# Output stores of four units with 8 KB rows in a scan and mixture-of-adapters kernel on one core

## The chip, the cores and the metric

The kernel runs on one core of one Trainium2 chip. The metric is the device time in microseconds (us) of one execution; less is better. The profile's span (200.2 us) is a little shorter than the device time, because it begins with the first instruction that the profiler records.

## What is computed

Two stages follow each other. The first is a linear recurrence over 6,400 time steps for 8 sequences of 128 channels; its result, seen as 51,200 rows of 128, goes through a mixture of 8 low-rank adapters of which each row uses its best two.

```python
# a, b: (8, 6400, 128) float32
h = np.zeros((B, D))
for t in range(S):
    h = a[:, t] * h + b[:, t]
    x[:, t] = h                          # x.reshape(51200, 128)
logits = x @ w_gate                      # (51200, 8)
topk = two largest logits of each row
w = softmax(the two logits)
delta = sum over the two e of  w_e * (x @ A[e]) @ B[e]   # A: 128x16, B: 16x128
out = x + delta                          # float32
```

The kernel must read a and b (26.2 MB each) and write out (26.2 MB): 78.6 MB in all, plus 0.14 MB of weights.

## The kernel before

The 51,200 rows are cut into 100 **units** of 512 rows. A unit goes through every engine. A small planner in the file lists all steps of all units as operations with their dependencies, gives each a key (`KEY`, one offset per kind of step), and lays them out as one fixed instruction order for each engine. On the chip each engine then works through its own list and waits on semaphores.

The steps of unit w, with the name that the planner has for each:

```python
load    SyncE    a, b of two units: HBM -> a_in, b_in, 512 KB each, rows of 4 KB
AB      TensorE  16 float32 transposes of a and b into two PSUM banks
aev     ScalarE  a: PSUM -> a_st              (ring of CFG["ast"] = 3)
scan    VectorE  tensor_tensor_scan           -> xT, float16 (ring of XR = 20 units)
ZL      TensorE  xT @ [w_gate | A]            -> PSUM;  zl (ScalarE) moves it to SBUF
gating  VectorE, GpSimd, ScalarE: top two of 8 logits and their weights, for groups of 3 units
mul     GpSimd (a few on VectorE): zw = z * weight
T       TensorE  transposes zw;  tev (VectorE, a few on ScalarE) moves it to SBUF
D       TensorE  x and zwT @ B added up in PSUM
oev     ScalarE  PSUM -> outt                 (ring of NOUT = 24 units)
store   SyncE    outt -> out, HBM
```

Rows go to partitions so that a store's rows are whole runs in HBM: a store of two units takes the 1,024 rows as `(p i) d -> p (i d)` with i = 8, so each of 128 partitions writes 8 rows of 128 floats, 4 KB in a row. For this, the matmul that reads xT picks every eighth row, and D of a unit can only run after the scan of both units of its pair:

```python
def x_block(v, q):
    if v in SOLO:
        x0 = (v % XR) * UT
        return xT[:, x0 : x0 + UT].rearrange("d (p i) -> d i p", i=Q)[:, q, :]
    x0 = (v - v % 2) % XR * UT
    return xT[:, x0 : x0 + 2 * UT].rearrange("d (p i) -> d i p", i=2 * Q)[:, v % 2 * Q + q, :]

def scanned(v):
    return f"scan{v if v in SOLO else v | 1}"

def readers(v):      # who must have read xT before scan(v + XR) writes there again
    both = [v] if v in SOLO else [v - v % 2, v | 1]
    return [f"D{u}" for u in both] + [f"ZL{k}" for u in both for k in fills_of.get(u, [])]
```

The stores. All loads and stores are issued on SyncE, in one order; a store of unit u0 is also held until the scan of unit u0 + HOLD (20), so that the loads go first and some stores are left for the end of the run:

```python
stores = [(u, 2) for u in range(0, NU - 2, 2)] + [(NU - 2, 1), (NU - 1, 1)]

def store(j):
    u0, n = stores[j]
    ...   # cut: source and destination views
    add_dma(f"st{j}", "sp", u0 + HOLD, [(rows, tile)], ("o", s0, n), ns,
            [f"oev{v}" for v in range(u0, u0 + n)] + [f"scan{min(u0 + HOLD, NU - 1)}"])
```

A load of unit w has key w - 16 in the same order and waits for AB of the units that had its place in the ring (8 places of two units, for a and for b). The three weight tensors are loaded on ScalarE's queue.

Of the kernel before, what the change touches and what calls it, by code (L numbers as in the profile page):

```python
# [12 lines left out]
CFG = {  # L13
    "ring": 8,
    "xr": 20,
    "zr": 48,
    "nout": 24,
    "hold": 20,
    "heads": (1, 1, 1, 1),
    "group": 3,  # L20
    "tails": (2, 2, 1, 1),
    "quick": (2, 2),
    "split": (4, 4),
    "solo": (2, 2),
    "mul": (0, 1, 0, 8),
    "tev": (1, 1, 4, 4),
    "tail": 8,
    "heat": 6,
    "filler": (2, 1, 1),
    "caps": {'a': 3, 'b': 4, 'Z': 1, 'O': 3, 'w': 8},  # L30
    "least": {'Z': 1, 'O': 1},
    "pairs": (98, 2),
    "ast": 3,
    "tevns": (264.0, 330.0),
    "key": {
        "AB": 170.4, "aev": 138.5, "scan": 13.3, "ZL": 157.0, "zl": 152.0, "gate": 31.6, "r1": -64.5, "r2": -65.8,
        "sig": 83.8, "mul": 73.7, "T": 119.3, "tev": 143.8, "D": 171.1, "oev": 151.4, "R": 65.1,
    },
}

# [60 lines left out]
class _Plan:  # L101
# [15 lines left out]
    def add(self, name, eng, kind, unit, busy, emit, deps=(), dma=None, mode=None, takes=(), gives=None):  # L117
        self.ops[name] = _Op(name, eng, kind, unit, busy, self.latency, emit, list(deps), dma, mode, takes, gives)
# [161 lines left out]
def bass_associative_scan_2x2__then__mixture_of_adapters_kernel(  # L280
# [8 lines left out]
    NB, S, D = a.shape  # L289
    E = moe_w_gate.shape[1]  # L290
    R = moe_A.shape[2]
# [4 lines left out]
    Q = 4  # L296
    UT = 64 * QI
    assert UT == 128 * Q and N % (2 * UT) == 0 and S >= UT
    NU = N // UT
    RING = CFG["ring"]  # L300
    XR = CFG["xr"]
    NOUT = CFG["nout"]
# [33 lines left out]
    GB = GM * Q  # L336
    SOLO = [v for v in range(NU) if v < CFG["solo"][0] or v >= NU - CFG["solo"][1]]
    assert CFG["solo"][0] % 2 == 0 and CFG["solo"][1] % 2 == 0 and XR % 2 == 0 and NOUT % 2 == 0
    p0, p1 = CFG["pairs"]
    PAIRED = {w: (w - p0) % 2 for w in range(p0, NU - p1)}  # L340
    assert (NU - p0 - p1) % 2 == 0 and p0 >= 2 and p1 >= 1
# [15 lines left out]
    fills_of = {}  # L357
# [11 lines left out]
    with ExitStack() as stack:  # L369
# [4 lines left out]
        cst_f = sb(nc.sbuf_tensor("cst_f", [128, E + 256], F32))  # L374
# [14 lines left out]
        xT = sb(nc.sbuf_tensor("xT", [128, XR * UT], F16))  # L389
        zw = [sb(nc.sbuf_tensor(f"zw{i}", [128, Q, 128], F16)) for i in range(NZW)]  # L390
        zwT = [sb(nc.sbuf_tensor(f"zwT{i}", [128, UT], F16)) for i in range(NZT)]
        zl = sb(nc.sbuf_tensor("zl", [128, ZR, E_A], F32))
        outt = sb(nc.sbuf_tensor("outt", [128, NOUT, UT], F32))
# [26 lines left out]
        def add_dma(name, eng, unit, starts, slot, ns, deps=(), kind="dma", issue=450.0, after=2000.0):  # L420

            if slot not in dma_sem:
                dma_sem[slot] = [sb(nc.semaphore("q_" + "_".join(map(str, slot)))), 0]
            dma_sem[slot][1] += 16 * len(starts)
            sem, value = dma_sem[slot]

            def emit(h):
                for dst, src in starts:
                    last = h.dma_start(dst, src).then_inc(sem, 16)
                return last  # L430

            add(name, eng, kind, unit, issue * len(starts), emit, deps, (sem, value, ns, after))
# [10 lines left out]
                out=ident_f[:, :],  # L443
# [7 lines left out]
            ["id0"],  # L451
        )

        add_dma("wg_in", "act", -110, [(cst_f[:, 0:E], moe_w_gate[:, :])], ("wg",), 80.0, (), "fix", 450.0, 2000.0)
        add_dma(
            "A_in",
            "act",
            -109,
            [(cst_f[:, E : E + 128], moe_A.rearrange("e (h l) r -> (e h) (l r)", l=8))],
            ("A",),  # L460
            220.0,
# [5 lines left out]
        add_dma(  # L467
            "B_in",
            "act",
            -108,  # L470
            [(cst_f[:, E + 128 : E + 256], moe_B.rearrange("e r d -> (e r) d"))],
            ("B",),
            220.0,
# [9 lines left out]
        def heat(h):  # L483
            for _ in range(CFG["heat"]):
# [13 lines left out]
                out=high[:, :], in_=ident_f[:, :].rearrange("p (e h) -> p h e", e=E), axis=AX.X, op=ALU.max  # L498
# [22 lines left out]
                out=mine[:, :], in_=ident_f[:, :].rearrange("p (e h) -> p e h", e=E), axis=AX.X, op=ALU.max  # L521
# [4 lines left out]
        for name, eng, lo, hi, time in (("spr0", "pool", 0, 3, 900.0), ("spr1", "dve", 3, 8, 760.0)):  # L526
# [7 lines left out]
                    out=spread[:, lo:hi, :, :],  # L534
# [61 lines left out]
        def place(t, w):  # L596

            shift = 1 if t == "a" else 0
            half = 64 * ((w + shift) % 2)
            return (w + shift) // 2, slice(half, half + 64)  # L600
# [7 lines left out]
        def column(t, w):  # L608

            return w * UT if t == "b" else 0  # L610

        def load(t, w):

            n = place(t, w)[0]
            many = 1 if (t, w) in alone else 2
            dst, i = rings[t][:, n % RING, :], QI
            if many == 1:
                dst, i = dst[:, column(t, w) : column(t, w) + UT], Q
            src = rows_of[t][w * UT : (w + many) * UT, :].rearrange("(p i) d -> p (i d)", i=i)
            for k in range(many):  # L620
                load_of[t, w + k] = f"ld{t}{w}"
            add_dma(
                f"ld{t}{w}",
                "sp",
                w - 2 * RING + (0 if w > 3 else -200),
                [(dst, src)],
                (t, n % RING, many, w if many == 1 else 0),
                1290.0 if many == 2 else 690.0,
                users.get((t, n - RING), []),
            )  # L630

        def transposes(w):
# [56 lines left out]
            )  # L689

        def readers(v):
            both = [v] if v in SOLO else [v - v % 2, v | 1]
            return [f"D{u}" for u in both] + [f"ZL{k}" for u in both for k in fills_of.get(u, [])]

        def scan(w):
            t0 = w * UT
# [6 lines left out]
            def emit(h):  # L703
# [21 lines left out]
                1187.0 + 130.0 * (len(cuts) - 2),  # L725
                emit,
                [f"AB{w}", f"aev{w}"] + [f"scan{w - 1}"] + readers(w - XR),
                gives=("b", w),
            )


        def x_block(v, q):
            if v in SOLO:
                x0 = (v % XR) * UT
                return xT[:, x0 : x0 + UT].rearrange("d (p i) -> d i p", i=Q)[:, q, :]
            x0 = (v - v % 2) % XR * UT
            return xT[:, x0 : x0 + 2 * UT].rearrange("d (p i) -> d i p", i=2 * Q)[:, v % 2 * Q + q, :]

        def scanned(v):
            return f"scan{v if v in SOLO else v | 1}"  # L740

        def products(k):
            b0, n = fills[k]
# [2 lines left out]
            def emit(h):  # L746
                for j in range(n):
                    dst = bank(("Z", k))[:, j * E_A : (j + 1) * E_A]
                    last = h.matmul(dst, x_block((b0 + j) // Q, (b0 + j) % Q), wA_h)
                return last  # L750
# [206 lines left out]
        def delta(v):  # L957
            def emit(h):
                for part in range(2):
                    for q in range(Q):  # L960
                        cols = slice(q * 128, (q + 1) * 128)
                        last = h.matmul(
                            bank(("O", v))[:, cols],
                            (x_block(v, q), zwT[v % NZT][:, cols])[part],
                            (ident_h[:, :], Bcat_h)[part],
                            start=part == 0 and q == 0,
                            stop=part == 1,
                            skip_group_check=True,
                        )
                return last  # L970

            add(f"D{v}", "pe", "D", v, 485.0, emit, [scanned(v), "idh", f"tev{v}", "cstB"], mode="full")
            plan.ops[f"D{v}"].at = {"cstB": Q}
# [15 lines left out]
                gives=("O", v),  # L989
            )  # L990

        stores = [(u, 2) for u in range(0, NU - 2, 2)] + [(NU - 2, 1), (NU - 1, 1)]
        store_of = {v: j for j, (u0, n) in enumerate(stores) for v in range(u0, u0 + n)}

        def store(j):
            u0, n = stores[j]
            s0 = u0 % NOUT
            rows = out[u0 * UT : (u0 + n) * UT, :]
            tile, ns = outt[:, s0 : s0 + n, :], 680.0 * n
            if u0 in SOLO:  # L1000
                rows = rows.rearrange("(n p i) d -> p n (i d)", p=128, i=Q)
            else:
                rows = rows.rearrange("(p i) d -> p (i d)", p=128)
                tile, ns = tile.rearrange("p n c -> p (n c)"), 1290.0
            add_dma(
                f"st{j}",
                "sp",
                u0 + HOLD,
                [(rows, tile)],
                ("o", s0, n),  # L1010
                ns,
                [f"oev{v}" for v in range(u0, u0 + n)] + [f"scan{min(u0 + HOLD, NU - 1)}"],
            )

        for w in range(NU):
            for t in "ab":
                if (t, w) not in load_of:
                    load(t, w)
# [15 lines left out]
            gating(k)  # L1034
        for j in range(len(stores)):
            store(j)
        ends = [f"st{j}" for j in range(len(stores) - NOUT, len(stores))]
        add("end", "sp", "fix", 1.0e9, 10.0, lambda h: h.nop(), ends)

        plan.schedule()  # L1040
# [49 lines left out]
```

## Time and profile before

| What | Value |
|---|---|
| Time, median of 3 runs | 201.86 us (201.60 to 201.91) |
| Span of the profiled run | 200.2 us |
| TensorE busy | 184.2 us (92%) |
| ScalarE busy | 180.0 us (90%) |
| VectorE busy | 173.8 us (87%) |
| GpSimd busy | 158.5 us (79%) |
| Mean DMA rate over the span | 396 GB/s |

How to read it: four compute engines have a high busy share, and the DMA engines a higher one. Busy time counts an instruction from its start to its end, and instructions of one engine overlap (100 `oev` copies of 625 ns and 100 `aev` copies of 628 ns stand for 61 us each), so a busy share of 90% is not the same as 90% of what the engine can do. The profile also cuts the span into slices and gives for each the share of the time in which the 16 DMA engines were busy and the GB/s that they moved; the share can come out a little over 1, because the packets of one engine overlap slightly.

### The profile page before, as it was taken

The numbers are of one execution on the slowest core, as the hardware profiler recorded it, in microseconds if no ns is written. First come the engines' busy times: TensorE is split into PE (matmuls) and PEld (weight loads), VectorE is DVE, ScalarE is ACT, GpSimd is POOL, SyncE is SP. The second block draws the span as 40 slices with busy tenths as digits, with TensorE's granted clock in tenths as the row PEclk, the third lists the DMA queues.
The fourth block names the chain that finished last, engine by engine and source line by source line (L and its number), as shares of the span: only waits on it lengthen the run. The fifth ranks groups of instructions, "written<-read, shape, count | busy, mean of one in ns | idle before, by whom it ended". The sixth has DMA issues, their size and how long they took to land.

```text
span 200.2 us, 8009 instructions
## 1 busy us (share of the span) xinstructions
PE 184.2 (92%) x3202; PEld 163.2 (82%) x3202; DVE 173.8 (87%) x302; ACT 180.0 (90%) x463; POOL 158.5 (79%) x278
## 2 busy tenths in 40 slices
PE   7599899999999999999989999999999999897760
PEld 3478797899998989999979998898899898796650
DVE  3369999999999999899989889879797999789950
ACT  3159999999999999999999999999999999999770
POOL 2315658889898999988789999999999898887720
PEclk9759999999999999999999999999999999999998
DMA  5999999999999999999999999999999999998994
GB/s 204 352 417 408 410 405 406 408 402 410 403 420 413 414 417 418 413 414 420 410 416 413 414 413 414 421 413 417 418 413 415 413 416 413 412 369 328 407 383 172
DMA packets 22629, 79.30 MB, mean 396 GB/s; under 512 B 2624, under 2 KB 2880, under 8 KB 22592
## 3 DMA queue, kind: packets, MB, share of 16 engines
q1 hardware_dynamic: 22160, 78.65, 97.8%
q8 instruction: 25, 0.41, 0.8%
q10 hardware_dynamic: 432, 0.14, 0.3%
q14 instruction: 12, 0.10, 0.1%
HBM read 52.56 MB, written 26.21 MB: 393 GB/s over the span
## 4 chain that ended last, share of the span: by engine, by line
PE 56%; DVE 22%; ACT 9%; DMA 3%; issue 3%; POOL 3%; POOLq 1%; SPq 0%; DVEq 0%; ACTq 0%
PE ps L94 29%; PE ps L98 28%; DVE xT L710 17%; ACT outt L978 3%; DMA a_in<-in_a_dram 3%; ACT a_st L686 3%; DVE zwT L942 2%; ACT zl L767 2%; POOL zw L926 2%; POOLq L369 1%; POOL d L880 1%; ACT pn L816 1%; DVE zw L926 1%; DVE m L851 1%; DVE m L873 0%
## 5 line engine op out<-in xcount | busy, mean ns | idle before, releaser
L710 DVE TENSOR_TENSOR_SCAN xT<-a_st,xT,ps 128x512 f16<-128x512 f32 x96 | 120.3, 1253 | 12.6 <-PE ps L98 6.2
L926 POOL TENSOR_TENSOR zw<-zl,g 128x512 f16<-128x512 f32 x93 | 99.2, 1072 | 8.5 <-ACT g L905 6.8
L767 ACT COPY zl<-ps 128x408 f32<-128x408 f32 (+1 forms) x139 | 73.0, 532 | 1.6 <-PE ps L94 1.6
L98 PE MATMUL ps<-ident_f,a_in 64*128 64x64 f32 (+1 forms) x792 | 68.7, 232 | 2.2 <-DMA a_in<-in_a_dram 2.2
L98 PE MATMUL ps<-ident_f,b_in 64*128 64x64 f32 (+1 forms) x792 | 67.4, 231 | 0.1
L686 ACT COPY a_st<-ps 128x512 f32<-128x512 f32 x100 | 60.9, 628 | 7.2 <-PE ps L98 6.2
L98 PEld LDWEIGHTS ps<-ident_f,a_in 64*128 64x128 f32 (+1 forms) x792 | 57.5, 141 | 9.5 <-DMA a_in<-in_a_dram 2.7
L978 ACT COPY outt<-ps 128x512 f32<-128x512 f32 x100 | 60.9, 625 | 2.0 <-PE ps L94 1.3
L98 PEld LDWEIGHTS ps<-ident_f,b_in 64*128 64x128 f32 (+1 forms) x792 | 56.5, 141 | 1.2 <-DVE xT L710 0.4
L94 PE MATMUL ps<-cst_h,xT 128*128 128x136 f16 x400 | 51.3, 236 | 1.0 <-DVE xT L710 0.5
L94 PE MATMUL ps<-ident_h,xT 128*128 128x128 f16 x400 | 42.5, 229 | 1.3 <-DVE zwT L942 1.0
L98 PE MATMUL ps<-ident_h,zw 128*128 128x128 f16 x400 | 39.1, 220 | 4.3 <-DVE zw L926 2.0
L94 PEld LDWEIGHTS ps<-cst_h,xT 128*128 128x128 f16 x400 | 36.4, 148 | 6.0 <-DVE xT L710 2.5
L94 PE MATMUL ps<-cst_h,zwT 128*128 128x128 f16 x400 | 38.7, 220 | 0.0
L942 DVE COPY zwT<-ps 128x256 f32<-128x256 f32 x89 | 35.7, 409 | 2.6 <-PE ps L98 2.4
L94 PEld LDWEIGHTS ps<-ident_h,xT 128*128 128x128 f16 x400 | 33.0, 147 | 3.4 <-DVE zwT L942 2.5
L98 PEld LDWEIGHTS ps<-ident_h,zw 128*128 128x128 f16 x400 | 25.0, 98 | 8.4 <-POOL zw L926 3.2
L94 PEld LDWEIGHTS ps<-cst_h,zwT 128*128 128x128 f16 x400 | 27.2, 99 | 0.0
L816 ACT ACTIVATE pn<-d 128x96 f32<-128x96 f32 (+2 forms) x72 | 22.6, 322 | 0.9 <-POOL d L858 0.6
L888 POOL TENSOR_TENSOR d<-d 128x96 f32<-128x96 f32 (+2 forms) x36 | 13.8, 383 | 5.0 <-DVE d L841 4.6
L866 POOL TENSOR_TENSOR L<-zl,pn 128x96 f32<-128x96 f32 (+2 forms) x34 | 12.9, 380 | 5.1 <-ACT pn L816 4.9
L880 POOL TENSOR_TENSOR d<-zl,m 128x96 f32<-128x96 f32 (+2 forms) x34 | 12.2, 359 | 4.7 <-DVE m L873 4.7
(38 smaller groups left out, 90.0 us busy)
## 6 DMA issues: line engine op xcount, KB each, us to landing
a_in<-in_a_dram SPq DMA_DIRECT2D x49, 512.0 KB, 15.3
b_in<-in_b_dram SPq DMA_DIRECT2D x49, 512.0 KB, 15.3
out_dram<-outt SPq DMA_DIRECT2D x49, 512.0 KB, 15.3
a_in<-in_a_dram SPq DMA_DIRECT2D x2, 256.0 KB, 8.9
b_in<-in_b_dram SPq DMA_DIRECT2D x2, 256.0 KB, 4.8
out_dram<-outt SPq DMA_DIRECT2D x2, 256.0 KB, 4.7
cst_f<-in_moe_A_dram ACTq DMA_DIRECT2D x1, 64.0 KB, 3.5
cst_f<-in_moe_B_dram ACTq DMA_DIRECT2D x1, 64.0 KB, 6.2
```

Source lines behind the costliest of these rows:

```text
L94: return self.handle.matmul(*args, **kwargs)
L98: return self.handle.transpose(*args, **kwargs)
L686: lambda h: h.copy(a_st[w % NAS][:, :], bank(("a", w))[:, :]),
L710: last = h.tensor_tensor_scan(out=x_at(lo, hi), data0=a_st[w % NAS][:, lo:hi], data1=bank(("b", w))[:, lo:hi], initial=init, op0=ALU.mult, ...
L767: return h.copy(zl[:, r0 : r0 + n, :], src)
L816: lambda h: h.activation(v(pn[s]), v(src[s]), ACTF.Relu, bias=bias, scale=scale),
L866: lambda h: h.tensor_tensor(out=v(L2[s]), in0=Lg, in1=v(pn[s]), op=ALU.subtract),
L880: lambda h: h.tensor_tensor(out=v(d2[s]), in0=Lg, in1=bc(m2[s]), op=ALU.subtract),
L888: lambda h: h.tensor_tensor(out=v(d1[s]), in0=v(d1[s]), in1=v(d2[s]), op=ALU.add),
L926: lambda h: h.tensor_tensor(out=oview, in0=zview, in1=gview, op=ALU.mult),
L942: return copy(zwT[v % NZT][:, :].bitcast(F32), bank(("O", v))[:, 0 : UT // 2])
L978: return copy(outt[:, v % NOUT, :], bank(("O", v))[:, :])
```

## The change

Stores become blocks of four units for units 4 to 91 (`quads` = (4, 8): not the first four, not the last eight). A block of four takes 2,048 rows with 16 rows to a partition, so each partition writes 8 KB in one run, and one DMA moves 1 MB. The other stores: two pairs at the start, three pairs and two single units at the end. This makes 29 stores in place of 51.

What comes with it:

- D of a unit must wait for the scan of the last unit of its block of four, and a place of xT becomes free only when all four units of its block have been read (`scanned`, `readers`, `x_block` by `block_of`).
- The output ring grows from 24 to 28 units, and `hold` from 20 to 22.
- a_st becomes a ring of 4 in place of 3.
- The weight loads stay on ScalarE's queue, with new keys.
- All keys are set anew, so every engine's list has another order. The split of work is moved a little: one in eight `tev` copies goes to ScalarE in place of all to VectorE; the gating groups at both ends have other sizes; more groups use the short way with `max` (7 in place of 4); the first units have more filler matmuls.

In the instruction lists: VectorE has 79 `tev` copies in place of 89 and 52 `max` in place of 16, ScalarE 21 `tev` copies in place of 11, SyncE 22 stores of 128 x 2048 floats and 5 of 128 x 1024 in place of 48 of 128 x 1024 and one with two 2 KB rows to a partition (units 0 and 1, which `solo` kept apart); the last two units have 128 x 512 in both. The matmuls of the computation are the same in number and shape.

```diff
-    "nout": 24,
-    "hold": 20,
-    "heads": (1, 1, 1, 1),
+    "nout": 28,
+    "hold": 22,
+    "quads": (4, 8),
+    "heads": (1, 2, 1),
     "group": 3,
-    "tails": (2, 2, 1, 1),
-    "quick": (2, 2),
-    "split": (4, 4),
-    "solo": (2, 2),
-    "mul": (0, 1, 0, 8),
-    "tev": (1, 1, 4, 4),
-    "tail": 8,
+    "tails": (2, 1),
+    "quick": (4, 3),
+    "split": (4, 8),
+    "solo": (0, 2),
+    "mul": (0, 1, 0, 10),
+    "tev": (7, 8, 4, 4),
+    "tail": 6,
     "heat": 6,
-    "filler": (2, 1, 1),
+    "filler": (2, 2, 2),
-    "ast": 3,
+    "ast": 4,
... (all of "key" set anew)
+    QUAD = range(CFG["quads"][0], NU - CFG["quads"][1])
+    def block_of(v):
+        n = 1 if v in SOLO else 4 if v in QUAD else 2
+        return v - v % n, n
... (keys of the weight loads; the planner's figure for how long a load takes)
         def readers(v):
-            both = [v] if v in SOLO else [v - v % 2, v | 1]
-            return [f"D{u}" for u in both] + [f"ZL{k}" for u in both for k in fills_of.get(u, [])]
+            if v < 0:
+                return []
+            u0, n = block_of(v)
+            whole = range(u0, u0 + n)
+            return [f"D{u}" for u in whole] + [f"ZL{k}" for u in whole for k in fills_of.get(u, [])]
... (x_block in the same way)
         def scanned(v):
-            return f"scan{v if v in SOLO else v | 1}"
+            u0, n = block_of(v)
+            return f"scan{u0 + n - 1}"
...
-        stores = [(u, 2) for u in range(0, NU - 2, 2)] + [(NU - 2, 1), (NU - 1, 1)]
+        stores = []
+        for v in range(NU):
+            u0, n = block_of(v)
+            if v == u0:
+                stores += [(v, n)]
...
+                        out[u0 * UT : (u0 + n) * UT, :].rearrange("(p i) d -> p (i d)", p=128),
+                        outt[:, s0 : s0 + n, :].rearrange("p n c -> p (n c)"),
```

More of the change, by code (lines that the diff above doesn't have):

```diff
@@ L32 @@
     "pairs": (98, 2),
-    "ast": 3,
+    "ast": 4,
     "tevns": (264.0, 330.0),
     "key": {
-        "AB": 170.4, "aev": 138.5, "scan": 13.3, "ZL": 157.0, "zl": 152.0, "gate": 31.6, "r1": -64.5, "r2": -65.8,
-        "sig": 83.8, "mul": 73.7, "T": 119.3, "tev": 143.8, "D": 171.1, "oev": 151.4, "R": 65.1,
+        "AB": 148.1, "aev": -10.9, "scan": -2.5, "ZL": -179.1, "zl": 147.2, "gate": -302.5, "r1": -175.8, "r2": 65.6,
+        "sig": -173.2, "mul": 90.5, "T": 106.8, "tev": 7.0, "D": 469.8, "oev": 384.8, "R": 65.09967571861861,
     },
@@ L338, in bass_associative_scan_2x2__then__mixture_of_adapters_kernel @@
     assert CFG["solo"][0] % 2 == 0 and CFG["solo"][1] % 2 == 0 and XR % 2 == 0 and NOUT % 2 == 0
+    QUAD = range(CFG["quads"][0], NU - CFG["quads"][1])
+    assert not QUAD or (XR % 4 == 0 and NOUT % 4 == 0 and QUAD[0] % 4 == 0 and len(QUAD) % 4 == 0)
+    def block_of(v):
+        n = 1 if v in SOLO else 4 if v in QUAD else 2
+        return v - v % n, n
     p0, p1 = CFG["pairs"]
@@ L452, in bass_associative_scan_2x2__then__mixture_of_adapters_kernel @@
         )
-        add_dma("wg_in", "act", -110, [(cst_f[:, 0:E], moe_w_gate[:, :])], ("wg",), 80.0, (), "fix", 450.0, 2000.0)
+        add_dma("wg_in", "act", -110.4, [(cst_f[:, 0:E], moe_w_gate[:, :])], ("wg",), 80.0, (), "fix", 450.0, 2000.0)
         add_dma(
@@ L457, in bass_associative_scan_2x2__then__mixture_of_adapters_kernel @@
             "act",
-            -109,
+            -107.5,
             [(cst_f[:, E : E + 128], moe_A.rearrange("e (h l) r -> (e h) (l r)", l=8))],
@@ L469, in bass_associative_scan_2x2__then__mixture_of_adapters_kernel @@
             "act",
-            -108,
+            -107.3,
             [(cst_f[:, E + 128 : E + 256], moe_B.rearrange("e r d -> (e r) d"))],
@@ L629, in load @@
                 users.get((t, n - RING), []),
+                after=2000.0 if many == 2 else 1250.0,
             )
@@ L732, in x_block @@
         def x_block(v, q):
[L733 to L737, printed above, removed]
+            u0, n = block_of(v)
+            x0 = u0 % XR * UT
+            return xT[:, x0 : x0 + n * UT].rearrange("d (p i) -> d i p", i=n * Q)[:, (v - u0) * Q + q, :]
         def scanned(v):
-            return f"scan{v if v in SOLO else v | 1}"
+            u0, n = block_of(v)
+            return f"scan{u0 + n - 1}"
         def products(k):
@@ L990, in o_evac @@
             )
-        stores = [(u, 2) for u in range(0, NU - 2, 2)] + [(NU - 2, 1), (NU - 1, 1)]
+        stores = []
+        for v in range(NU):
+            u0, n = block_of(v)
+            if v == u0:
+                stores += [(v, n)]
         store_of = {v: j for j, (u0, n) in enumerate(stores) for v in range(u0, u0 + n)}
@@ L997, in store @@
             s0 = u0 % NOUT
[L998 to L1004, printed above, removed]
             add_dma(
@@ L1008, in store @@
                 u0 + HOLD,
-                [(rows, tile)],
+                [
+                    (
+                        out[u0 * UT : (u0 + n) * UT, :].rearrange("(p i) d -> p (i d)", p=128),
+                        outt[:, s0 : s0 + n, :].rearrange("p n c -> p (n c)"),
+                    )
+                ],
                 ("o", s0, n),
-                ns,
+                {1: 690.0, 2: 1290.0, 4: 2510.0}[n],
                 [f"oev{v}" for v in range(u0, u0 + n)] + [f"scan{min(u0 + HOLD, NU - 1)}"],
@@ L1036, in bass_associative_scan_2x2__then__mixture_of_adapters_kernel @@
             store(j)
-        ends = [f"st{j}" for j in range(len(stores) - NOUT, len(stores))]
+        ends = [f"st{j}" for j in range(len(stores))]
         add("end", "sp", "fix", 1.0e9, 10.0, lambda h: h.nop(), ends)
```

## The prediction, written before the changed kernel was run

> **What bounds the kernel now.** I read the page's slices of the span and its DMA queues first, because four engines above 79% busy do not tell which of them sets the pace.
>
> ```profile
> DMA  5999999999999999999999999999999999998994
> GB/s 204 352 417 408 410 405 406 408 402 410 403 420 413 414 417 418 413 414 420 410 416 413 414 413 414 421 413 417 418 413 415 413 416 413 412 369 328 407 383 172
> DMA packets 22629, 79.30 MB, mean 396 GB/s; under 512 B 2624, under 2 KB 2880, under 8 KB 22592
> ## 3 DMA queue, kind: packets, MB, share of 16 engines
> q1 hardware_dynamic: 22160, 78.65, 97.8%
> ...
> q10 hardware_dynamic: 432, 0.14, 0.3%
> ```
>
> SyncE's queue (q1) keeps the 16 DMA engines busy for 97.8% of the span. From slice 3 to slice 35 the rate hardly moves, about 403 to 420 GB/s. Only the start, slices 36 and 37 (369 and 328 GB/s) and the very end are lower. So the run is a full DMA pipe of some 165 us with a ramp ahead of it, a **dip** at 175 to 185 us, and a tail. The busy time by stretches of 2 us shows the dip and the tail. After the label the columns are the length, then busy us and instructions of PE, PEld, DVE, ACT and POOL, then the TensorE clock, the DMA share and GB/s.
>
> ```profile
> 174.00:176.00 2.00, 1.35 (x18) 1.14 (x19) 2.00 (x3) 1.63 (x5) 1.77 (x4) 1.00 1.02 406
> 176.00:178.00 2.00, 2.00 (x47) 1.86 (x45) 1.37 (x5) 1.86 (x5) 1.69 (x3) 1.00 0.94 381
> 178.00:180.00 2.00, 2.00 (x33) 1.99 (x31) 2.00 (x4) 2.00 (x6) 2.00 (x3) 1.00 0.85 346
> 180.00:182.00 2.00, 2.00 (x32) 1.83 (x31) 2.00 (x5) 2.00 (x7) 1.26 (x5) 1.00 0.69 268
> 182.00:184.00 2.00, 1.20 (x19) 0.95 (x16) 1.86 (x5) 1.92 (x7) 1.35 (x4) 1.00 0.82 332
> 184.00:186.00 2.00, 1.43 (x19) 1.10 (x20) 2.00 (x7) 1.39 (x6) 2.00 (x4) 1.00 1.02 406
> ...
> 194.00:196.00 2.00, 0.35 (x7) 0.18 (x4) 0.00 (x0) 0.91 (x2) 0.00 (x0) 1.00 0.83 323
> 196.00:198.00 2.00, 0.00 (x0) 0.00 (x0) 0.00 (x0) 0.00 (x0) 0.00 (x0) 1.00 0.66 258
> ```
>
> A full pipe has a share of about 1.025. In the four stretches from 176 to 184 us, 2 x (0.085 + 0.175 + 0.335 + 0.205) = 1.6 us of transfer time is missing. Who holds the stores back is in the waits of SyncE's queue:
>
> ```profile
> SPq L248 <- DVE xT L710: 15.0, 6, 4.1
> ...
> SPq L248 <- DMA out_dram<-outt: 4.0, 5, 1.2
> ```
>
> Line 248 is the explicit wait ahead of an instruction. Six times, 15 us in all, SyncE waits for a scan (L710): these are stores held until the scan of unit u0 + 20. By the issue times the last of them leave at 168.9, 173.4, 176.6, 180.9 and 182.9 us, and the backlog in front of the DMA engines is used up meanwhile. The waits that the same view books on the issue line itself (58.7 us of them to PE) I read as the full pipe holding SyncE, since the places they could wait for had long been free: a load takes 15.3 us from issue to landing (median), which is twelve transfers of about 1.27 us.
>
> The compute engines follow the pipe closely but do not set it. The transposes of the last units begin 3.0 to 4.1 us after their loads landed (the load with b of units 98 and 99 landed at 173.6, the transposes of unit 98 begin near 177), and PE waits for a load once, for 2.7 us, at the start. At the end they matter: the last load lands at 175.6, the last scan begins at 181.6, the last output copy (oev of unit 99) at 194.4, and the last store is issued at 195.0 and lands at 199.7 us.
>
> **What the Trainium skill says.** "DMA: Bandwidth & Descriptors", section "Where 436 GB/s comes from", puts the ceiling of the 16 engines at 435 GB/s, 27.2 bytes per ns for one. The trace agrees. Its packet records, grouped by size, have medians of 159 ns for 4 KB (18,688 packets), 84 ns for 2 KB, 27 ns for 512 B and 9 ns for the 4-byte completion that ends a transfer on each engine. From 2 to 4 KB it is 75 ns for 2,048 bytes, 27.3 bytes per ns. That leaves a fixed 9 ns for a packet. The same page, "Why small descriptors are slow (HBM only)", tells of a fixed cost of about 3 cycles per packet inside the engine; at that ceiling's 850 MHz I estimate 3.5 ns from it, so the trace shows the kind of cost but at 9 ns, and I use the 9. The section "Issuing engines are not separate DMA queues" says that transfers from ScalarE run on the same engines and save only issue time. The trace agrees: q10 (the weights) takes 0.3%. Their new keys should be worth nothing.
>
> **The change, part by part.**
>
> *8 KB rows.* Two pair stores cost one DMA engine 16 packets x 159 ns + 2 completions x 9 ns = 2,562 ns. One store of four costs 8 x (9 + 2 x 150) + 9 = 2,481 ns. The 8 KB packets that the runtime itself moves in this trace (19 of them) have a median of 319 ns and reach down to 309 at the tenth percentile, which fits. So 81 ns less each, 22 times: **1.78 us**. The first store loses its 2 KB rows: 16 x 84 - 8 x 159 = 72 ns. Together 1.85 us of engine time; at a share of 1.025 that is 1.8 us of the pipe. Nothing of it is hidden as long as the pipe is full. The author's planner has 2,510 ns for a store of four and 1,290 for a pair: 70 ns, 1.5 us. I take 1.5 to 1.8.
>
> *How much reaches the last load.* In both SyncE lists 64 units of stores stand ahead of the last load and 36 after it. Ahead of it now stand 15 blocks of four: 15 x 81 ns = 1.2 us. The last load should land near 174.3.
>
> *Hold 22 and 28 places.* After the last load, blocks at 64, 68, 72, 76 and 80 wait for scans 86, 90, 94, 98 and 99. Before, the pair at 76 waited for scan 96 (175.2 us) and the one at 78 for scan 98 (179.6). Now all four units wait for scan 98. This alone would deepen the dip. Against it: in the new TensorE list 13 D stand after the transposes of unit 99, before 11. Scans run two units further ahead of the outputs, while loads come 1.2 us earlier and units have 3 to 4 us in stock, so scan 98 can begin 2 to 3 us earlier, at about 177. The 12 units at 64 to 75 last 12 x 0.635 = 7.6 us after the last load's bytes. I expect half of the dip to go: **0.8 us**.
>
> *The coupling to blocks of four.* scan(w) may now need D of unit w - 17, before w - 19. In the middle of the run 17 to 18 scans have begun past a unit when its output copy starts (oev of unit 40 starts at 99.6 us, its scan at 70.8), so this will bind there and hold scans back by a unit or two, some 2 to 3 us. A place of the ring is free about 10 us before its next load leaves SyncE (the transposes of units 63 and 64 begin at 109 to 111 us, their place's next load is issued at 121.8 us), so the pipe should not notice.
>
> *Work moved.* 10 tev copies at 409 ns leave VectorE and 36 more max of about 88 ns (16 took 1.4 us) come: -4.1 + 3.2, with 10 small reductions of 0.23 us fewer as well, about -3 us in all. ScalarE gains 10 copies of 390 ns. None of it is on the pipe. At the end the sign turns: after the last scan VectorE has 24 max in place of 8, 1.4 us more, though the short way has no relu round trips.
>
> *Sum.* The last transfer cannot finish earlier than compute allows: last load 1.2 us earlier and the same 19.4 us to the last store's issue gives 193.8. Its 4.7 us to landing hold some backlog (the first load of this size took 2.9 us); with the backlog gone, about 1 us is won there. On the DMA side the end moves by 1.8 + 0.8 = 2.6 us; on the compute side by 1.2 + 1.0 = 2.2 us, or less if the tail's gating is slower. I choose 2.1 us: 201.86 - 2.1 = **199.8 us**.
>
> **Rivals.** *The compute tail takes over:* the pipe finishes its 1.8 us early and idles until the last outputs. For it: oev 99 at 194.4 stands close to the end already, and more of VectorE's work lies after the last scan. Then the gain is 0.5 to 1 us, 201 us. *Blocks of four starve something:* a block waits for its fourth output and a later scan, the dip grows to 3 us, or the coupling w - 17 slows the middle. For it: the lag of 17 to 18 units. Against it: the full backlog. It would make 201.5 to 203 us. *The whole dip goes and the tail shortens too,* as the new order was set for this: 1.8 + 1.6 + 1 = 4.4 us, 197.5 us. *8 KB packets are no cheaper:* against it stand the four sizes on one straight line. It would leave 201 us.
>
> **Range and chances.** The saving in packets is the firm part; the end of the run decides the rest, either way. 8 in 10: 197.9 to 201.6 us. Faster by over 2% means under 197.8, which needs nearly everything: 0.09. Slower by over 2% (over 205.9) needs a starved pipe for 4 us and more: 0.02.
>
> **What would show it.** Packets of q1 near 22,160 - 22 x 128 - 22 x 16 - 128 = 18,900. A median near 309 ns for 8 KB. Full slices at 416 to 420 GB/s where they were 413 to 417. The last load landing near 174.3. The dip half as deep. The last store issued near 193.8 us. If 8 KB packets take 318 ns the first step is wrong; if the slices at 175 to 185 us are as low as before, or the last store is issued at 195 us or later, the third is.

## The result, and the profile after

The changed kernel takes 200.88 us (median of 4 runs, 200.84 to 200.97) where the kernel before takes 201.76: a ratio of 0.9957, 95% interval 0.9940 to 0.9974. A repeat of 22 runs on another occasion gave 201.17 us and 0.9994 (0.9976 to 1.0011). So the gain is small, between nothing and 0.9 us. The prediction said 2.1 us.

The slices and queues of the changed kernel's page, first as in the prediction:

```profile
DMA  5999999999999999999999999999999999989984
GB/s 218 393 416 407 412 406 402 410 407 406 408 414 421 414 418 421 415 416 419 412 416 422 413 411 416 419 415 417 421 415 416 417 416 414 422 348 411 392 328 170
DMA packets 19333, 79.29 MB, mean 398 GB/s; under 512 B 2272, under 2 KB 2528, under 8 KB 16480
## 3 DMA queue, kind: packets, MB, share of 16 engines
q1 hardware_dynamic: 18864, 78.65, 97.3%
q8 instruction: 25, 0.41, 0.8%
```

The packets are as expected: 18,864 on q1, and 8 KB packets of 309 ns in the median. Yet the busy share of q1 fell only from 97.8% to 97.3%, and the full slices from the twelfth on run at 411 to 422 GB/s, hardly more than before (between 60 and 170 us the mean is 417 for 415 GB/s). The second slice is better (393 for 352 GB/s), long before the first store. The dip is still there, with a second one behind it:

```profile
174.00:176.00 2.00, 1.77 (x26) 1.60 (x24) 2.00 (x5) 1.62 (x6) 2.00 (x4) 1.00 0.92 381
176.00:178.00 2.00, 2.00 (x33) 1.93 (x32) 2.00 (x6) 2.00 (x8) 1.49 (x4) 1.00 0.74 311
178.00:180.00 2.00, 1.91 (x30) 1.70 (x29) 1.72 (x4) 1.75 (x6) 2.00 (x3) 1.00 0.92 373
...
186.00:188.00 2.00, 1.77 (x24) 1.21 (x21) 2.00 (x4) 1.37 (x6) 1.61 (x2) 1.00 0.85 356
...
190.00:192.00 2.00, 1.46 (x22) 1.13 (x21) 1.39 (x3) 1.92 (x7) 0.33 (x2) 1.00 0.61 238
```

The columns are those of the prediction's table. By its own reckoning (0.1 + 0.29 + 0.1 in the first dip, 0.17 and 0.41 in the later ones, times 2 us) over 2 us of transfer time are missing, more than the 1.6 us before. (All ten stretches from 174 to 194 us together give 2.6 us now, 1.6 us before.) SyncE's explicit waits for scans grew with it, from 15.0 to 20.0 us, in fewer and longer pieces:

```profile
SPq L249 <- DVE xT L723: 20.0, 4, 8.7
```

The dip grew, then, and the time still fell a little. Cheaper packets could have paid for a costlier dip, so this alone does not show that the dip is harmless; the landing records show why it may be. A transfer is complete when all 16 DMA engines have added their one to its semaphore; the Trainium skill ("DMA: Bandwidth & Descriptors", section "Why a DMA increments its semaphore by 16 and not by 1") says that they finish independently, and the trace agrees. Of each transfer I took the first and the last of the 16 landings. What lies between them is how far the slowest engine is behind the fastest, called the **lag** from here on. The columns give the time of the first landing:

| Kernel | about 25 us | about 100 us | about 160 us |
|---|---|---|---|
| before | 2.6 us | 4.1 us | 5.8 us |
| changed | 2.0 us | 3.5 us | 5.8 us |

At the last load the fastest engine is done at 168.6 and the slowest at 174.9 us (changed). From there the slowest lands a block of four every 2.6 to 2.7 us, at 177.55, 180.27, 182.94, 185.53, 188.25, 190.89 and 193.51 us, right through both dips. The packet records agree: from 172 to 196 us there is no moment at which fewer than two of the 16 engines have a packet (four in the kernel before). So in a dip only the engines that are ahead stand idle. The reading is this: **the engine that is furthest behind never runs dry, and it ends the run**; the mean busy share does not show it. The packet records do not name the engine, so that it is one and the same engine throughout is not shown. The experiments test this reading.

In the same stretch the fastest engines land a block every 2.4 to 2.5 us (171.05, 173.50, 175.92 us). The slowest therefore loses a further 0.2 us or so with each block; why, no record here shows. In experiment 9 it stops when the compute does.

### The profile page after: what moved, and what is told of

It is laid out like the page before. It is cut to its first block, busy times and chain, and to the rows that moved or that the text cites. A ratio compares the mean times of both kernels' runs of the same rounds, so it can differ in the third digit from the quotient of the medians.

```text
span 199.1 us, 7930 instructions
## 1 busy us (share of the span) xinstructions
PE 184.5 (93%) x3204; PEld 163.7 (82%) x3204; DVE 173.0 (87%) x320; ACT 179.3 (90%) x466; POOL 153.8 (77%) x264
## 3 DMA queue, kind: packets, MB, share of 16 engines
q1 hardware_dynamic: 18864, 78.65, 97.3%
## 4 chain that ended last, share of the span: by engine, by line
PE 40%; ACT 21%; DVE 21%; DMA 6%; issue 4%; POOL 3%; SPq 2%; POOLq 0%; DVEq 0%; ACTq 0%
PE ps L99 20%; PE ps L95 19%; DVE xT L723 14%; ACT a_st L696 7%; DMA b_in<-in_b_dram 6%; ACT outt L990 6%; ACT zl L779 5%; DVE zwT L954 3%; SPq L438 2%; ACT pn L828 2%; POOL zw L938 2%; ACT g L917 1%; DVE um L907 1%; DVE mx L834 1%; ACT zwT L954 1%
## 5 line engine op out<-in xcount | busy, mean ns | idle before, releaser
L938 POOL TENSOR_TENSOR zw<-zl,g 128x512 f16<-128x512 f32 x92 | 97.8, 1066 | 12.0 <-ACT g L917 10.1
L779 ACT COPY zl<-ps 128x408 f32<-128x408 f32 (+1 forms) x142 | 76.1, 560 | 0.3 <-PE ps L95 0.3
L696 ACT COPY a_st<-ps 128x512 f32<-128x512 f32 x100 | 62.7, 673 | 7.5 <-PE ps L99 7.0
L99 PE MATMUL ps<-ident_f,a_in 64*128 64x64 f32 (+1 forms) x792 | 67.8, 230 | 1.5 <-DMA a_in<-in_a_dram 1.3
L99 PE MATMUL ps<-ident_f,b_in 64*128 64x64 f32 (+1 forms) x792 | 66.2, 230 | 1.4 <-DMA b_in<-in_b_dram 1.2
L990 ACT COPY outt<-ps 128x512 f32<-128x512 f32 x99 | 65.5, 669 | 1.5 <-PE ps L95 1.0
L954 DVE COPY zwT<-ps 128x256 f32<-128x256 f32 x79 | 31.3, 410 | 2.5 <-PE ps L99 2.4
L828 ACT ACTIVATE pn<-d 128x96 f32<-128x96 f32 (+1 forms) x65 | 23.1, 366 | 1.1 <-POOL d L844 0.6
L917 ACT ACTIVATE g<-um 128x96 f32<-128x96 f32 (+2 forms) x36 | 12.7, 353 | 1.5 <-DVE um L907 1.4
L907 POOL TENSOR_TENSOR um<-d,pn 128x96 f32<-128x96 f32 x30 | 11.7, 390 | 2.9 <-ACT pn L828 2.5
```

Of the source, the lines that this page charges most:

```text
L99: return self.handle.transpose(*args, **kwargs)
L696: lambda h: h.copy(a_st[w % NAS][:, :], bank(("a", w))[:, :]),
L779: return h.copy(zl[:, r0 : r0 + n, :], src)
L828: lambda h: h.activation(v(pn[s]), v(src[s]), ACTF.Relu, bias=bias, scale=scale),
L907: lambda h: h.tensor_tensor(out=v(um[s]), in0=v(d1[s]), in1=v(pn[s]), op=ALU.subtract),
L917: lambda h: h.activation(v(g[k % 3]), v(um[s]), ACTF.Sigmoid),
```

## The experiments

**1 and 2. The pipe alone.** All compute is left out: SyncE issues the loads and stores of one kernel, in that kernel's order, from a cleared buffer. Nothing is computed, so the output is only zeros.

```diff
-        @block.tensor, scalar, vector, gpsimd: all compute
+        for t, u, n in jobs:     # SyncE's list of before, or of the changed kernel
+            wait for the transfer 8 places earlier of this tensor; dma_start(...)
```

> No compute at all: the loads and stores of the kernel before, in the order of its SyncE list, stores of two units with 4 KB rows, from a cleared buffer. It measures what the pipe alone takes: 78.65 MB at the 413 to 417 GB/s of the full slices is 189 to 190 us, with 2 us of clearing, 2 us until the first packet and 2 to 3 us after the last about 195 us. Both theories expect the same here.

> The same with the changed kernel's list: 22 stores of four units with 8 KB rows. Theory A, the prediction's: each packet costs the engine its full 9 ns beyond its bytes, so this is 1.8 us shorter than the pairs alone. Theory B: packets of one engine overlap (the shares of 1.02 to 1.03), so part of the 9 ns was never paid, and it is 0.6 to 0.9 us shorter.

Measured: pairs 198.63 us (ratio to the kernel before 0.9849, 0.9824 to 0.9873), blocks of four 198.26 us (0.9837, 0.9818 to 0.9856). The difference of 0.4 us is not resolved, but 1.8 us (0.009 in the ratio) is well outside. Theory A, the prediction's, falls here. The 195 us was too low: the first transfer is issued at 3.0 us, behind the clearing, where the kernel's is at 0.7 us, and the device time is 1.8 us longer than the span (197.84 for 196.0 us in the profiled run).

```profile
DMA  1999999999999999999999999999999999999995
GB/s 61 328 408 416 409 412 408 409 410 410 411 417 420 420 420 422 415 421 419 419 420 419 420 421 418 421 418 422 420 418 424 417 420 420 419 420 419 421 420 219
...
q1 hardware_dynamic: 22032, 78.65, 99.1%
```

This is the page of the pipe with pairs. No dip, and every slice full to the last but one. The slowest engine is 1.5 us behind at 25, 100 and 160 us alike: the lag is made in the first 10 us and does not grow.

With blocks of four the pipe does not stay so even: the lag is 1.3 us at 25, 2.0 at 100, 2.5 at 160 and 3.1 us at the end. Against the pairs the fastest engine ends 0.94 us earlier (192.70 for 193.64 us) and the slowest 0.57 us later (195.76 for 195.19 us). So even the fastest engine gains half of the 1.78 us, and the growing lag hides that gain. Its cause is not known.

The packets of the last us of the kernel before, when one engine is left, show the true price of one: 2 KB packets of 84 ns begin **80 ns** apart, and a completion of 9 ns holds up the next packet for 6. Each packet overlaps its neighbour by about 4 ns. With 75 ns for 2,048 bytes that leaves 5 ns and not 9, and a block of four saves 8 x 5 + 6 = **46 ns** and not 81. The end of the pipe, where only stores are left, agrees: the slowest engine lands a store of two units every 1,242 ns and a store of four every 2,442 ns, so a store of four saves 2 x 1,242 - 2,442 = 42 ns.

**3. The changed kernel with pairs.**

```diff
-    "quads": (4, 8),
+    "quads": (0, 100),
```

> The changed kernel with stores of two units everywhere, all else as in it (ring of 28, hold 22, keys, gating groups). Theory of the tail (VectorE's work after the last scan sets the end, the packets saved do not reach it): within 0.5 us of the changed kernel, 200.4 to 201.4 us. Theory of the pipe (the packets saved are what made it faster): 1.2 to 1.8 us slower than the changed kernel, 202.1 to 202.7 us, no better than before.

Measured: 201.68 us, ratio 1.0003 (0.9991 to 1.0014). Ring, hold, keys and groups bring nothing by themselves. Against the changed kernel's 0.9957 the blocks bring 0.9 us, against its repeat (0.9994) 0.2. It fits neither expectation: between the two, and near the kernel before.

**4. The kernel before with blocks of four.**

```diff
     (CFG of before)
+    "quads": (4, 8),
-    "solo": (2, 2),
+    "solo": (0, 2),
... (block_of and what goes with it, and the keys of the weight loads, as in the changed kernel)
```

> The kernel before with stores of four for units 4 to 91 alone: hold 20, 24 places, the old keys and groups. If the coupling (a scan needs D of 17 units earlier, D needs the scan of the last unit of four) is felt by the old order, scans and outputs wait for each other and it takes 204 to 210 us. If the full pipe hides it, as the prediction had it, 200.5 to 201.5 us.

Measured: 212.76 us, ratio 1.0532 (1.0468 to 1.0595). The coupling is felt, beyond the range expected, at the end of the run:

```profile
GB/s 223 408 410 411 406 410 404 407 406 408 413 420 421 407 414 417 415 413 419 412 420 421 410 421 413 415 413 424 417 416 418 418 416 404 322 159 117 2 281 320
```

Up to slice 33 the pipe is full; then the outputs are missing, down to 2 GB/s. The output of unit 80 comes 29 us behind its scan, before 21 us, and after the last scan at 178.4 us it takes 27 us until the last output, before 12.8. So the blocks need what came with them in the changed kernel (order, ring and `hold` together; which of these was not tested). Here the lack is far longer than the slowest engine's lag, which falls to 0.2 us: between 172 and 206 us there are 10.1 us in which none of the 16 engines has a packet, and the run takes 11 us longer.

**5 and 6. Smaller and larger rows in the pipe alone.**

```diff
-    ... o0:2 o2:2 ...             pairs, 4 KB rows
+    ... o0:1 o1:1 o2:1 o3:1 ...   one unit, 2 KB rows
+    ... o0:8 ...                  eight units, 16 KB rows (second kernel)
```

> The pipe alone with every store cut to one unit, 2 KB rows: 100 stores in place of 51. Each pair that is cut in two costs one DMA engine 8 more packets and one more completion. Theory A (each costs 9 ns in full): 49 x 81 ns = 4.0 us more than the pipe with pairs, 202.6 us. Theory B (half of it is hidden by overlap, 26 to 50 ns for each cut): 1.3 to 2.5 us more, 199.9 to 201.1 us.

> The pipe alone with stores of eight units, 16 KB rows, for units 0 to 95: 36 fewer packets' worth of eight and 36 fewer completions than with pairs. Theory A: 36 x 81 ns = 2.9 us less than pairs, 195.7 us. Theory B: 0.9 to 1.8 us less, 196.8 to 197.7 us.

Measured: 200.59 us (0.9939, 0.9915 to 0.9963) and 197.80 us (0.9806, 0.9782 to 0.9830). Against the pairs that is +2.0 us for 49 cuts, 40 ns each, and -0.8 us for 36 joins, 23 ns each. The intervals of the ratios make this 23 to 51 ns for a cut and 5 to 43 ns for a join: 46 ns lies inside the first and just above the second, and 81 ns lies outside both, so A is excluded twice more. At the end of these pipes, where only stores are left, a store of one unit takes 645 ns and one of eight 4,847 ns. There a cut costs 48 ns and a further doubling of the rows brings 37 ns. Why the stores of eight bring less over the whole run is open. The page of the skill from which the prediction took 3 cycles ("Why small descriptors are slow (HBM only)"), 3.5 ns by its estimate, was nearer than the 9 ns read from durations: measured 5 ns.

**7 and 8. The pipe beside a TensorE instruction stream.** 3,200 matmuls run on TensorE and touch none of the pipe's data; then half as many, each twice as wide.

```diff
+        @block.tensor
+        def _(h):
+            for _ in range(3200):     # second kernel: 1600, 256 columns
+                h.matmul(ps[:, 0:128], wt[:, :], wt[:, :])
```

> The pipe with pairs, and beside it 3,200 matmuls on TensorE that touch none of its data. In the profiles of both kernels 25 packets of 16 KB come in on queue 8 during the run, and the slowest of the 16 DMA engines falls 6 us behind the fastest, which it does not in the pipe alone. Theory of the slowest engine (fetching TensorE's instructions takes DMA time, unevenly, and every transfer ends with its slowest engine): 25 such packets again, the lag grows to 4 to 6 us and the time by 2 to 4 us, 200.6 to 202.6 us. Theory of the compute tail alone (the difference between the pipe and the kernel is made by compute at the end): no change, 198.3 to 198.9 us.

> The pipe with pairs and a TensorE stream of half as many instructions, each twice as long (1,600 matmuls of 256 columns): the same TensorE time with half the code. Theory of the slowest engine, by instruction fetch: 12 or 13 packets of 16 KB in place of 25, and half of the 4.2 us that the full stream cost, 200.2 to 201.2 us. If it is TensorE's running itself (power, memory) that slows the pipe: 202.8 us again.

Measured: 202.81 us (1.0052, 1.0029 to 1.0076) and 199.90 us (0.9916, 0.9885 to 0.9948), where the pipe alone takes 198.63. The queue lines of the two pages:

```profile
q1 hardware_dynamic: 22032, 78.65, 97.6%
q8 instruction: 25, 0.41, 0.8%
```

```profile
q1 hardware_dynamic: 22032, 78.65, 98.4%
q8 instruction: 12, 0.20, 0.4%
```

Queue 8 carries TensorE's own program: it has 25 packets, 12, or none where TensorE does nothing. "Runtime: NRT & Kernel Launch", section "Instruction fetch mechanics", of the skill says that it comes in blocks of 16 KiB, 256 instructions each. The trace agrees: the kernels' 6,400 or so TensorE instructions (3,202 matmuls and as many weight loads before) are 25 packets of 16 KB, each of about 1.03 us. The page also calls the cost mostly hidden; no run here shows this for the engine that executes the code. The DMA engines of a full pipe do not hide it: 202.81 us stand for 198.63.

With 25 packets the lag of the slowest engine grows from 1.9 us at 26 us to 4.9 at 162 and 5.3 at the end; with 12 it ends at 3.4; with pairs and none it stays at 1.5. In the full stream the fastest engine ends 0.5 us later than in the pipe alone (194.17 for 193.64 us) and the slowest 4.3 us later (199.50 for 195.19 us). With nearly the same TensorE busy time (176.5 for 180.7 us) half the code costs 1.3 us in place of 4.2; the intervals, 0.5 to 2.2 and 3.4 to 4.8 us, let a half in.

So TensorE's running as such does not cost this time. The number of matmuls and weight loads was halved with the code, and the times alone do not separate the two; the landings do. In the half stream a fetch comes every 14 us. Between 14 and 190 us the lag grows by 0.1 us or more in one step 8 times, and 7 of these steps come 2.1 to 3.0 us after a fetch has begun. The pipe with pairs alone has no such step.

**9. The outputs at the end made earlier.** Gating, weights and adapters are left out for units 91 to 99; their outputs are x alone.

```diff
-            z_mul(v); zw_tr(v); t_evac(v)
+            if v < CUT:                        # 91
+                z_mul(v); zw_tr(v); t_evac(v)
-                for part in range(2):
+                for part in range(2 if v < CUT else 1):
... (gating of these groups left out too)
```

> The changed kernel without gating, weights and adapters for units 91 to 99 (their outputs are x alone): the outputs at the end come some 4 us earlier, nothing else is changed. Theory of the compute tail: 2 to 4 us less than the changed kernel, 197 to 199 us. Theory of the slowest DMA engine (it has not been idle since the start, whatever the others do): at most 0.5 us less, 200.4 to 200.9 us.

Measured: 200.87 us, ratio 0.9965 (0.9951 to 0.9979), against 0.9957 and 0.9994 in the two measurements of the changed kernel: between nothing and 0.6 us less, though the last output copy starts at 185.1 us in place of 193.5. The busy times, in stretches of 2 us:

```profile
184.00:186.00 2.00, 0.00 (x0) 0.00 (x0) 0.00 (x0) 1.90 (x4) 0.00 (x0) 1.00 1.00 418
186.00:188.00 2.00, 0.00 (x0) 0.00 (x0) 0.00 (x0) 0.00 (x0) 0.00 (x0) 0.90 1.04 434
...
192.00:194.00 2.00, 0.00 (x0) 0.00 (x0) 0.00 (x0) 0.00 (x0) 0.00 (x0) 0.50 1.00 395
194.00:196.00 2.00, 0.00 (x0) 0.00 (x0) 0.00 (x0) 0.00 (x0) 0.00 (x0) 0.50 0.37 143
```

No engine computes after 186 us, and the pipe goes on, full to 194 us, then down to the slow engines; the last landing is at 197.9 us, 0.7 us before the changed kernel's. The rival of the compute tail, 2 to 4 us, falls. What there is to gain came by way of the slowest engine: once compute is over it lands a block every 2.45 to 2.49 us, where it took 2.58 to 2.73 us before.

**10. Blocks of four beside the full stream.** Experiment 7 with the changed kernel's list.

> The changed kernel's list with the full TensorE stream of 3,200 matmuls. Theory B (a packet costs 5 ns and a completion 6 ns of an engine's time beyond the bytes, 46 ns for each block of four): 22 x 46 ns = 1.0 us less than the pairs with the same stream, which took 202.8 us, so 201.5 to 202.1 us. Theory A (81 ns each): 201.0 us or less.

Measured: 201.67 us, ratio 0.9999 (0.9986 to 1.0011), 1.1 us less than the pairs with the same stream (1.0052). By the intervals it is 0.5 to 1.6 us less: the 22 x 46 = 1,012 ns lie inside, A's 1.78 us outside. It is the one place where the worth of blocks of four is clear of the spread.

**11 to 13. The depth of the dip.**

```diff
-    "hold": 22,
+    "hold": 24,      # second kernel: 20; third: the changed kernel again
```

> The changed kernel with stores held for 24 scans in place of 22: four more units of stores stand behind the last load, which lands about 2.5 us earlier, and the pipe's dip moves and deepens. If the dip costs time, as the prediction had it, this is 0.5 us or more slower or faster with the depth of the dip. Theory of the slowest engine: the dip is time in which only the engines that are ahead idle, the slowest has the same packets to move, so within 0.3 us of the changed kernel, 200.6 to 201.2 us.

> The changed kernel once more, on the same chip and against the same runs as the next one, since the run with hold 24 was compared with it across two calls. Both theories: 200.7 to 201.0 us where the kernel before takes 201.6 to 201.8, a ratio of 0.9957 within its interval.

> The changed kernel with hold 20 in place of 22: the same order of transfers behind the last load (12 stores, 36 units), but the blocks at 64 to 76 may leave two scans earlier, so the dip is shallower. If the depth of the dip costs time (hold 24 had the deeper dip and a ratio of 0.9996): 0.3 to 0.6 us faster than the changed kernel in the same call, 200.2 to 200.6 us, and faster than both. If only the slowest engine's packets count: within 0.3 us of it.

Measured: hold 24: 201.37 us, 0.9996 (0.9983 to 1.0008); the changed kernel again: 201.17 us, 0.9994 (0.9976 to 1.0011); hold 20: 201.86 us, 1.0001 (0.9981 to 1.0020). The first two lines are of hold 24, the last two of hold 20:

```profile
176.00:178.00 2.00, 1.77 (x25) 1.46 (x23) 1.80 (x13) 2.00 (x6) 2.00 (x3) 1.00 0.78 324
178.00:180.00 2.00, 2.00 (x34) 1.86 (x32) 1.97 (x8) 1.82 (x8) 1.51 (x5) 1.00 0.55 225
...
176.00:178.00 2.00, 2.00 (x37) 1.86 (x35) 1.92 (x3) 2.00 (x7) 2.00 (x5) 1.00 0.75 315
...
182.00:184.00 2.00, 1.30 (x19) 0.97 (x16) 2.00 (x6) 2.00 (x8) 1.65 (x3) 1.00 0.42 172
```

Against the expectation hold 20 has the deepest stretch of all, 0.42. By the prediction's reckoning, from 174 to 194 us, the transfer time that is missing is 1.6 us in the kernel before, 2.6 in the changed kernel, 3.0 in its repeat, 1.9 with hold 24 and 2.7 with hold 20. With hold 20, too, at least one engine has a packet at every moment up to 196 us. The times do not follow the missing time: the repeat, which misses 1.4 us more than the kernel before, is not slower, and the three ratios are the same within their intervals. By the medians hold 20 is 0.7 us behind the repeat, so a cost of some tenths of a us is not excluded.

The last store with hold 24 is issued 1.4 us earlier than the changed kernel's (192.7 for 194.1 us) and lands no earlier (199.0 for 198.6). That hold 20 would beat both kernels did not come true, and the repeat shows that the first 0.9957 was at the good end.

## Why the prediction was wrong

- **What bounds the kernel**: right in that the full pipe does, wrong in what ends the run. It named a mean share of 16 engines. The end is set by the slowest of them, which is 5.8 us behind at 160 us.
- **"81 ns less each, 22 times: 1.78 us"**: this step failed in its size. It added up packet durations. Durations overlap, which the share of 1.025 said plainly; dividing the saving by 1.025 was not enough, since the overlap is about 4 ns for each packet, nearly half of the 9. Measured: 46 ns by the distance of packet starts, 42 ns where only stores are left, 40 and 23 ns over the whole run by the smaller and larger rows, 1.1 us for all 22 with a full instruction stream. The planner's 70 ns was too high as well.
- **"How much reaches the last load"**: 0.7 us (174.85 for 175.59) in place of 1.2. Even that cannot be put down to the blocks: at the load of units 19 and 20, before any store, the slowest engine was already 1.0 us earlier (31.3 for 32.4 us).
- **"I expect half of the dip to go: 0.8 us"**: this step failed in kind. The missing transfer time grew from 1.6 to 2.6 us, and no run shows that it costs time, since the slowest engine does not run dry in it (experiments 9 and 11 to 13). That scan 98 would begin near 177 us was right (176.4), and of no use.
- **The coupling to blocks of four**: rightly hidden in the changed kernel. With the old order it cost 11 us.
- **The sum on the compute side** (last store issued at 193.8 us): right, 194.1. But compute does not set the end; the last store lands 4.5 us after its issue in place of 3.7, and in experiment 9 it is issued 5.8 us earlier (188.3 us) for at most 0.7 us.
- **What is left of the sum**: with 46 ns for 81 and nothing for the dip, 1.0 us stands in place of the 2.6 us of the DMA side and of the 2.1 us chosen. The two measurements, 0.9 and 0.1 us by their ratios, lie below that.

What stays open: where the rest of the 1.0 us is lost in the changed kernel's repeat (0.3 us by the medians). One candidate is the growing lag that blocks of four show in the pipe alone. Another is the start of a run, which varies by as much: in the eight profiled runs with compute SyncE's queue has moved between 2.61 and 2.97 MB in the first 10 us, which is 0.9 us of the pipe. The three of them under 2.75 MB (hold 20, the kernel before, the changed kernel with pairs) took 201.69 to 201.99 us. Of the five above 2.9 MB, the four other than experiment 4 took 200.60 to 201.35 us. This fits, but these are different kernels, and the other timed runs have no packet records, so it is argued and not shown.

## What to carry to other kernels

When the DMA engines are the bound, read the first and the last of each transfer's 16 landings: here the engine that was furthest behind set the end. Dips in the mean share of up to 3.0 us of missing transfer time, and a last output 8 us earlier, moved the time by no more than some tenths of a us while that engine did not run dry (experiments 9 and 11 to 13); once it did, the lack cost its full 11 us (experiment 4). Price a packet by the distance between packet starts and not by its duration. In a full pipe the program of TensorE is DMA traffic too: halving it was worth 2.9 us in the pipe alone, larger rows 1.1 us. Fewer instructions were not tried in the kernel itself.

## What the runs showed of the hardware that was not expected

- 25 instruction fetches of 16 KB, 0.5% of the bytes, cost the pipe 4.2 us (202.81 for 198.63 us), and unevenly: the fastest engine ends 0.5 us later, the slowest 4.3 us.
- In the pipe with pairs a lag of 1.5 us from the first 10 us stood unchanged for 180 us. With blocks of four and no fetch at all it grew from 1.3 to 3.1 us, which is unexplained.
- The pipe without any compute takes 198.3 to 198.6 us, with a start 2.3 us later than the kernel's. From the same start all the compute of the kernel before would cost about 5.3 us beside its transfers (an estimate: 201.6 - 198.6 + 2.3); the TensorE stream alone cost the pipe 4.2 us.
